# A hand-written order of operations changed in the first four steps, and the last output store split by columns

## The chip, the cores and the metric

The kernel runs on one core of one Trainium2 chip. The metric is the device time of one execution in microseconds (us); the time before is the median of three runs. Five engines work side by side, each through its own queue in order: TensorE (PE in the profile, its weight loads PEld), VectorE (DVE), ScalarE (ACT), GpSimd (POOL) and SyncE (SP), which here only issues DMAs. ACT and POOL issue DMAs too, from the same queues as their other work.

## The reference

```python
f = 1.0 / (1.0 + np.exp(-f_logit))                      # (4, 8, 768, 48)
state = np.zeros((B, H, D, D))
for t in range(S):
    state = f[:, :, t, :, None] * state + einsum('bhd,bhe->bhde', k[:, :, t], v[:, :, t])
    y[:, :, t] = einsum('bhd,bhde->bhe', q[:, :, t], state)
x = y.transpose(0, 2, 1, 3).reshape(3072, 384)
h = x @ w_in                                            # (3072, 2048)
g = np.maximum(h, 0.0) + alpha * np.minimum(h, 0.0)
out = g @ w_out                                         # (3072, 384)
```

All is float32: 4 batches, 8 heads of 48, 768 positions; then a network of width 2048 with a slope alpha for negative values.

## The kernel before

**Steps.** The positions are cut into 6 chunks of 128, the batches into 2 pairs: 12 steps (`STEPS`), each one chunk of one pair, 256 rows of the output. Steps 0 and 1 are the first chunk of the two pairs. In a step three parts are defined as a table of small named operations, `w[name]`: `preparation` (load, sigmoid, products of gates, scaled q and k), `attention` (scores, state, output y) and `network` (the two matrix products).

**Words of the order.** A word stands for one or a few instructions. In `preparation`: `ld.0` to `ld.4` load f, q, k and the two halves of v; `sg`, `kr`, `qc`, `c0` to `c3`, `cg` are ACT's sigmoid and copies; `l1` to `l3`, `le`, `e2` to `e7`, `nr`, `gk`, `k4`, `ke`, `sa`, `sb` are elementwise products on DVE or POOL (all from one helper line, L235); `sc` are scans on DVE, `fs` the factors of the state; `kt` transposes the scaled keys on DVE and `km` moves the pieces with 16 DMAs of SP (L492). `zi` to `zd`, `ci`, `co`, `ch`, `cq`, `cd`, `mr`, `bl` are constants made on POOL. In `attention`: `r` raw scores, `x` scores between groups of four, `h` between halves, `of` blocks off the diagonal, `kp`, `pd`, `pz` key transposes and state products, `y` outputs, `t` the layout of y (all PE); `R`, `X`, `H`, `oc`, `p`, `m`, `z`, `T` copy their results; `mv` moves y into xT by DMA. In `network`: `n0` to `n7` are first-layer products (12 rows of PE each in the profile, `na` and `nb` of step 0 have 24), `g` ACT's negative part, `G` DVE's gates; then seven products by quarters of the second layer, `A1`, `A2`, `B`, `C1`, `C2`, `D`, `E`, over sums of gates `S0`, `S1` and differences of weights `W` (so 7 products in place of 8); `ka`, `u2`, `u3`, `d0`, `oa`, `b`, `d1`, `e` add them up. `d1` and `e` each end with the store of 128 rows of the output. Step 0 has its own network: `na`, `nb`, `ga`, `Ga`, `va`, `vb`, `o`. In step 0, `a` and `b` behind a word mark the two batches of the pair, done apart. `id`, `ih`, `il`, `ib` and `jd`, `jh`, `jl`, `jb` load w_in and w_out in eight pieces each and turn them into the layout of the kernel (DMA, two ACT passes, one DVE sum). `iq`, `ik`, `is`, `ip`, `ix` with a number are products whose results nobody uses.

**The order.** The whole program is one list, `ORDER` (L93): the text `FIRST` for steps 0 to 3 and the parts of steps 3 and 4 that fall between, then `USUAL` repeated for steps 4 to 12, with `+` and `-` for the next and the step before. A word carries its step behind the colon; a last letter V, G or A chooses the engine (DVE, POOL, ACT; for a load the queue of SP, POOL or ACT). The loop at L962 emits the words one after the other, so each engine's queue is the list cut down to its words, and an instruction waits for the tiles that it reads and for the buffers that it takes. The first word on each engine that can't run holds all behind it.

**Buffers.** f, q, k and most tiles of `preparation` have one buffer each (`mine`, `bufs=1`), so a load waits for the last reader of the step before. PSUM: two pairs of banks (`psa`) for scores, state and y, and four single banks (`psn`) for the network; the first of those can be had only when `psf`, the pool of the opening, is given back. Five raw buffers hold pieces of the weights.

The change touches `FIRST` (L31 to L67) and, in `network`, `store`, `oa` and `last`.

## Time and profile before

| what | value |
|---|---|
| runs | 611.93 us median of 3 (611.59 to 613.8) |
| profiled execution | 614.22 us, of it 612.4 us span |
| PE busy | 587.3 us, 96% |
| DVE busy | 488.6 us, 80% |
| ACT, POOL busy | 241.6 and 101.2 us, 39% and 17% |
| chain that ended last | PE 78%, DVE 1% |
| mean granted TensorE clock | 0.986 |
| DMA | 50.41 MB, 82 GB/s mean |

The page cuts the span into 40 slices of 15.3 us; a digit is the busy share in tenths.

```profile
PE   1799899989999999999999999999999999999997
DVE  7978899995857799899899899899889889762251
POOL 4706564364441000000000000000000000000000
PEclk9869999989999999999999999999999999999999
```

POOL works in the first 13 slices alone: the steps of `FIRST` use it for products beside DVE, `USUAL` does not. The clock that the throttle granted is below full in the second, third and ninth slice. Steps of `USUAL` take 46.9 us each (the first `n0` of steps 4 and 5 at 196.36 and 243.21 in the chain of waits). A busy row of PE is not PE at its peak, since its matmuls are pipelined; where it has no gap at all, though, what starts later there ends later.

### The profile page before, as it was taken

What the parts mean: (1) busy time and instruction counts of PE and PEld (TensorE: products, weight loads), DVE (VectorE), ACT (ScalarE), POOL (GpSimd) and SP (SyncE); (2) the same over time, 40 slices, a digit from 0 to 9 for tenths busy, and PEclk for the clock granted to TensorE, in tenths of its full rate; (3) what the DMA queues carried; (4) which work ended last, traced back from release to release, by engine and by line L of the source; (5) the groups of instructions that cost most, each with busy time, mean ns of one, the idle gap of its engine ahead of it and who ended that gap; (6) DMA issues with size and microseconds to landing.
All of it is one profiled execution on the core that took longest, in us unless ns stands there. A gap on an engine that the chain in (4) does not pass through costs nothing.

```text
span 612.4 us, 18785 instructions
## 1 busy us (share of the span) xinstructions
PE 587.3 (96%) x8036; PEld 529.5 (86%) x8036; DVE 488.6 (80%) x996; ACT 241.6 (39%) x461; POOL 101.2 (17%) x141
## 2 busy tenths in 40 slices
PE   1799899989999999999999999999999999999997
PEld 1789857879999899899899899899889889889997
DVE  7978899995857799899899899899889889762251
ACT  5669853414330361272271261261362263223110
POOL 4706564364441000000000000000000000000000
PEclk9869999989999999999999999999999999999999
DMA  8866472223001602502602602502601601201000
GB/s 296 255 208 230 130 232 68 78 47 72 3 29 35 165 8 50 161 2 47 164 1 44 166 2 44 167 1 40 165 7 39 166 7 36 46 3 27 26 1 27
DMA packets 73555, 50.41 MB, mean 82 GB/s; under 512 B 47248, under 2 KB 63120, under 8 KB 73472
## 3 DMA queue, kind: packets, MB, share of 16 engines
q1 hardware_dynamic: 66080, 39.63, 24.2%
q10 hardware_dynamic: 6064, 6.69, 3.7%
q0 software_dynamic: 1328, 2.89, 1.8%
q8 instruction: 64, 1.05, 0.7%
q14 instruction: 19, 0.16, 0.1%
HBM read 36.21 MB, written 4.72 MB: 67 GB/s over the span
## 4 chain that ended last, share of the span: by engine, by line
PE 78%; DVE 1%; issue 0%
PE ph L799 35%; PE pc L894 10%; PE pa L894 9%; PE pe L894 5%; PE pd L894 5%; PE pb L894 4%; PE py L730 3%; PE qu L537 3%; PE raw L517 2%; PE state L655 1%; PE off L617 1%; DVE ss L380 0%; DVE vs L691 0%; DVE o L898 0%; DVE y L739 0%; DVE q L235 0%
## 5 line engine op out<-in xcount | busy, mean ns | idle before, releaser
L799 PE MATMUL ph<-xT,w_in_sb 128*128 128x256 f32 x1056 | 238.0, 384 | 0.0
L799 PEld LDWEIGHTS ph<-xT,w_in_sb 128*128 128x128 f32 x1056 | 199.2, 191 | 29.9 <-issue 1.9
L809 DVE SCALAR_TENSOR_TENSOR gate<-neg,om,ph 128x256 f32<-128x256 f32 x176 | 76.3, 477 | 48.2 <-ACT neg L805 47.0
L805 ACT ACTIVATE neg<-ph 128x512 f32<-128x512 f32 x88 | 51.9, 598 | 158.5 <-PE ph L799 130.4
L767 POOL DMA_DIRECT2D xT<-y x22 | 11.9, 545 | 366.0 <-ACT y L739 366.0
L894 PE MATMUL pc<-t,S 128*128 128x192 f32 x352 | 61.8, 329 | 0.2 <-DVE o L898 0.2
L894 PE MATMUL pa<-w_out_sb,gate 128*128 128x192 f32 x352 | 61.9, 328 | 0.0
L894 PEld LDWEIGHTS pa<-w_out_sb,gate 128*128 128x128 f32 x352 | 57.8, 190 | 1.8 <-DVE gate L809 1.2
L894 PEld LDWEIGHTS pc<-t,S 128*128 128x128 f32 x352 | 57.3, 190 | 1.2 <-DVE o L898 0.5
L544 DVE COPY_PREDICATED ad<-mquad,qu 128x160 f32<-128x160 int32 (+6 forms) x140 | 41.9, 300 | 10.8 <-PE qu L537 5.0
L524 DVE COPY_PREDICATED ad<-mraw,raw 128x128 f32<-128x128 int32 (+3 forms) x96 | 41.6, 442 | 3.8 <-POOL fs L235 0.9
L453 ACT COPY A<-q 48x512 f32<-48x512 f32 x40 | 24.7, 618 | 41.8 <-DVE q L235 41.4
L368 ACT COPY ut<-qd 128x256 f32<-128x256 f32 (+1 forms) x52 | 31.8, 631 | 21.5 <-DVE qd L235 10.2
L235 DVE TENSOR_TENSOR ut<-ut,fs 128x128 f32<-128x128 f32 (+6 forms) x63 | 36.8, 588 | 0.7
L517 PE MATMUL raw<-qd,k 48*32 48x80 f32 x1536 | 23.0, 244 | 13.6 <-DVE qd L235 11.1
L517 PEld LDWEIGHTS raw<-qd,k 48*32 48x32 f32 x1536 | 18.2, 109 | 19.3 <-ACT ut L370 11.1
L917 ACT ACTIVATE o<-pa 128x192 f32<-128x192 f32 x11 | 3.6, 330 | 72.6 <-PE pa L894 72.6
L716 ACT COPY A<-ad 32x256 f32<-32x256 f32 x75 | 30.0, 401 | 2.5 <-DVE ad L544 1.3
L898 DVE SCALAR_TENSOR_TENSOR Csum<-pc,Csum 128x192 f32<-128x192 f32 x22 | 7.9, 357 | 28.6 <-PE pc L894 28.4
L894 PE MATMUL pe<-w_out_sb,S 128*128 128x192 f32 x176 | 30.4, 326 | 0.0
L894 PE MATMUL pb<-t,gate 128*128 128x192 f32 x176 | 30.4, 326 | 0.0
L894 PE MATMUL pd<-w_out_sb,S 128*128 128x192 f32 x176 | 30.4, 326 | 0.0
(138 smaller groups left out, 852.6 us busy)
## 6 DMA issues: line engine op xcount, KB each, us to landing
f<-in_fT SPq DMA_DIRECT2D x11, 512.0 KB, 3.9
w_in_raw<-in_w_in SPq DMA_DIRECT2D x7, 767.2 KB, 7.0
q<-in_qT SPq DMA_DIRECT2D x10, 512.0 KB, 4.9
out<-o SPq DMA_DIRECT2D x24, 192.0 KB, 2.1
k<-in_kT SPq DMA_DIRECT2D x8, 512.0 KB, 7.0
vs<-in_v SPq DMA_DIRECT2D x18, 192.0 KB, 6.9
w_out_raw<-in_w_out SPq DMA_DIRECT2D x4, 767.8 KB, 5.7
w_out_raw<-in_w_out ACTq DMA_DIRECT2D x4, 767.8 KB, 5.6
```

Of the source, the lines that this page charges most:

```text
L235: (nc.gpsimd if beside[0] else nc.vector).tensor_tensor(*a)
L368: w[f"c{r}{mark}"] = lambda r=r: nc.scalar.copy(q4()[:, gs, :, r], qdv[r][:, gs, :, 0])
L453: copy(A[halves(cc)[1], u0:u1, par * HP:(par + 1) * HP, CH * cc:CH * (cc + 1)], x["q3"][rows(par)].rearrange("p (u h c) s t -> p u h c (s ...
L517: nc.tensor.matmul(to[DB * j:DB * (j + 1), par, hp * C:hp * C + QW], lhsT=x["k"][r_, g * DB:(g + 1) * DB], rhs=qd[r_, g], start=True, stop ...
L524: nc.vector.copy_predicated(adu[:, :, :, d:4], mraw[:, d, :, d:4].bitcast(I32).unsqueeze(1).broadcast_to((128, H, NB, n_)), rv[:, :, QO[d] ...
L537: nc.tensor.matmul(to[DB * j:DB * (j + 1), par, o + 4:o + width], lhsT=x["k4"][r_, g * DB:(g + 1) * DB], rhs=x["us"]()[r_, g, 4:width], st ...
L544: nc.vector.copy_predicated(ad[:, u, :, :, 4 * m:DB], mquad[:, lo:lo + n_].bitcast(I32).unsqueeze(1).unsqueeze(1).broadcast_to((128, 2, HP ...
L716: copy(A[s_, u, :, s_], ad[s_, u].rearrange("p r h t -> p (r h) t"))
L799: nc.tensor.matmul(ph[f][:, j * T:(j + 1) * T], lhsT=w_in_sb[:, kt, m * 128:(m + 1) * 128], rhs=x["T"][:, kt], start=(kt == 0 and j == 0), ...
L805: nc.scalar.activation(neg[f], ph[f].rearrange("p (j t) -> p j t", j=2), AF.Relu, scale=-1.0)
L809: nc.vector.scalar_tensor_tensor(gate[:, m % NH, m // NH], neg[f][:, j], om[:, m:m + 1], ph[f].rearrange("p (j t) -> p j t", j=2)[:, j], A ...
L894: nc.tensor.matmul(p[name][:, 0:DH], lhsT=of(f), rhs=by(f), start=(f == 0 and not more), stop=(f == NH - 1), skip_group_check=True)
```

## The change

`FIRST` is replaced by another list of nearly the same words. Of 738 entries, five products without use leave and eight come (`iq.23`, `iq.25`, `iq.27`, `is.8`, `ip.3` against `ik.0`, `ik.2`, `iq.6`, `iq.15`, `iq.22`, `ip.7`, `ix.10`, `ix.11`), and 75 words change engine or queue:

```
step 0: V to G gkb.0 lea nrb.2 sbb.1 sba.1 p01; G to V l3b.0 saa p10; V to A T01 T10 jd7; A to V ldb.3 jd6
step 1: V to G l2.1 ld.3 S0.1; G to V gk.1 ke.0 gk.3 p01 S1.0 S1.1 S1.2; A to V p13 p02; V to A z0; G to A p10; A to G p11
step 2: V to G ld.4 l1.1 l2.0 p13 S0.2 S1.3; G to V l1.0 k4 sb.1 p02 p12 S0.0; A to V p10; A to G p03 p11 p00; G to A ld.2 p01
step 3: V to G k4 sb.1 e2 ld.4 sb.0 p02; G to V ld.2 l1.1 l3.0 sa e5 p13 p01; V to A ld.0 ld.3 z0; A to V p03 z1
step 4: V to G l3.0 k4 le e5 e6; G to V ld.3 l1.1 e3 sa ke.2
```

The rest is shifted places. Below are the parts of the list around the opening, around the products of step 1, and at its end, before and after, then the code.

```diff
@@ -31,40 +31,40 @@
 FIRST = """
-zi:0 ms:0 al:0 zv1:0 zm:0 zk:0 ldb.0V:0 zv0:0 ldb.1V:0 sgb:0 ci:0 l1b.0V:0 l2b.0V:0 mr.2:0 zo.0:0 zf:0 zo.1:0 l3b.0G:0 qcb:0 lda.0V:0 l1b.1V:0 sga:0
-l1a.0V:0 kra:0 krb:0 ldb.2V:0 l2a.0V:0 lda.1V:0 qca:0 l2b.1V:0 zA:0 c2b:0 l3a.0V:0 l1a.1V:0 c0a:0 lda.2V:0 k4aV:0 l2a.1V:0 c2a:0 ch.0:0 sca.1:0 cga:0
-id3A:0 l3b.1V:0 r1:0 k4bV:0 c0b:0 scb.1:0 gka.0V:0 cgb:0 l3a.1V:0 c3a:0 ldb.4V:0 id0V:0 gkb.0V:0 sca.0:0 mr.0:0 id5V:0 bl:0 gkb.1V:0 c1a:0 gka.1V:0
-id4V:0 ih0:0 kea.1V:0 ih5:0 cq.0:0 iq:0 cq.6:0 c1b:0 r0:0 gkb.2V:0 gka.2V:0 cq.4:0 leaV:0 ch.4:0 keb.0V:0 gka.3V:0 h0:0 c3b:0 zd:0 il0:0 kea.0V:0
-lebV:0 gkb.3V:0 H0.0:0 kea.2V:0 nra.0G:0 lda.4A:0 cd.0:0 nrb.0V:0 scb.0:0 sabV:0 sbb.0G:0 keb.2V:0 cd.1:0 keb.1V:0 fs:0 nrb.1V:0 mr.3:0 nrb.2V:0
-ldb.3A:0 nra.1V:0 mr.1:0 sbb.1V:0 nra.2G:0 co:0 h1:0 H1.0:0 H1.1:0 ch.1:0 kpa:0 kpb:0 sba.1V:0 ch.5:0 ch.2:0 il4:0 iq.23:0 H0.2:0 iq.24:0 iq.25:0
-H0.1:0 R0.0:0 ch.3:0 H1.2:0 R1.0:0 R1.1:0 R1.2:0 R1.3:0 ih3:0 cq.1:0 R0.1:0 R0.2:0 kca:0 cd.2:0 ld.0V:1 sg:1 ih4:0 iq.27:0 ld.1V:1 R0.3:0 kcb:0 x1:0
-x0:0 X0.0:0 ofb:0 il3:0 saaG:0 X0.1:0 ofa:0 X1.0:0 qc:1 oc1b:0 is.8:0 ch.6:0 l1.0G:1 pzb:0 lda.3V:0 pza:0 oc0a:0 pda:0 pdb:0 X0.2:0 X1.1:0 p00V:0
-oc1a:0 p02V:0 p01V:0 p03V:0 m0a:0 s10b:0 m0b:0 X1.2:0 oc0b:0 sba.0G:0 s11b:0 l1.1V:1 ip.3:0 s11a:0 p12V:0 s10a:0 bl:1 ib0V:0 y0:0 z0A:0 id1V:0 p11A:0
-il1:0 ih1:0 p13G:0 kr:1 t0:0 T02A:0 jd5A:0 ib4V:0 l2.0V:1 id2V:0 ih2:0 il2:0 id7V:0 T00V:0 p10G:0 y1:0 ib1V:0 T01V:0 na0:0 z1A:0 t1:0 ld.2G:1 l2.1V:1
...
-g4:1 G4.1:1 m1.2:2 G4.0:1 n2:1 ke.1G:3 ke.2V:3 kt:3 km:3 r1:3 R1.0:3 g2:1 W20G:0 r0:3 n1:2 S1.0G:1 S1.2G:1 g1:2 ld.4V:3 n0:2 G3.1:1 e3V:3 e4G:3 e5G:3
-e6G:3 e7G:3 G3.0:1 G2.0:1 G2.1:1 R0.0:3 R1.1:3 R0.1:3 A1:1 ka:1 R1.2:3 R1.3:3 S0.0V:1 S0.1V:1 S0.3V:1 g0:2 sg:4 kr:4 B:1 fs:3 S0.2V:1 G0.0:2 R0.2:3
-R0.3:3 A2:1 n4:2 l1.0G:4 G0.1:2 G1.0:2 x0:3 X0.0:3 qc:4 oa:1 ld.2V:4 l1.1G:4 l2.1G:4 X0.1:3 X0.2:3 S1.1G:1 X0.3:3 X0.4:3 l2.0V:4 G1.1:2 sb.0V:3
-ld.4G:4 x1:3 X1.0:3 C1:1 X1.1:3 S1.3G:1 g4:2 n2:2 X1.2:3 X1.3:3 u2:1 C2:1 G4.1:2 m0.0:3 X1.4:3 X1.5:3 pd:3 X1.6:3 s01:3 p13G:3 of:3 s11:3 c0:4 p11V:3
...
-m1.1:3 e:1 d1:1 ka:2 ke.2G:4 A2:2 z1A:3 u2:2 mv:3 e4V:4 e5V:4 D:2 d0:2 S1.3V:2 E:2 oa:2 e6V:4 S1.2V:2 e7V:4 m1.2:3 C2:2 ke.1G:4 kt:4 km:4 fs:4 u3:2
-b:2 d1:2 e:2 s10:4
+zi:0 ms:0 al:0 cq.0:0 ci:0 zv1:0 ch.0:0 ldb.0V:0 zv0:0 ik.0:0 zf:0 ldb.1V:0 sgb:0 l1b.0V:0 lda.0V:0 qcb:0 l2b.0V:0 l1b.1V:0 zm:0 lda.1V:0 c0b:0 cd.0:0
+cd.1:0 l3b.0V:0 mr.2:0 l2b.1V:0 sga:0 l1a.0V:0 zk:0 l3b.1V:0 kra:0 mr.3:0 cgb:0 lda.2V:0 qca:0 c0a:0 zA:0 gkb.0G:0 zo.0:0 l2a.0V:0 zo.1:0 l3a.0V:0
+l1a.1V:0 ldb.2V:0 r1:0 cga:0 gka.0V:0 id3A:0 lda.4A:0 id0V:0 sca.0:0 l2a.1V:0 l3a.1V:0 r0:0 iq:0 gka.1V:0 c2a:0 k4aV:0 c3a:0 scb.1:0 krb:0 k4bV:0
+c3b:0 mr.0:0 bl:0 sca.1:0 kea.1V:0 c2b:0 c1a:0 leaG:0 mr.1:0 zd:0 id5V:0 gka.2V:0 gka.3V:0 ih5:0 h0:0 c1b:0 iq.24:0 lebV:0 keb.0V:0 ch.1:0 gkb.1V:0
+nrb.1V:0 nra.0G:0 gkb.2V:0 kea.0V:0 gkb.3V:0 H0.0:0 ldb.4V:0 ik.2:0 ih0:0 il0:0 nrb.0V:0 nrb.2G:0 ch.3:0 keb.1V:0 H0.1:0 id4V:0 il4:0 H0.2:0 h1:0
+H1.0:0 kea.2V:0 scb.0:0 ldb.3V:0 keb.2V:0 cd.2:0 sabV:0 nra.1V:0 cq.6:0 fs:0 R0.0:0 R0.1:0 R0.2:0 ih3:0 ld.0V:1 sbb.0G:0 H1.1:0 iq.6:0 ch.6:0 ch.5:0
+kpa:0 sbb.1G:0 H1.2:0 ch.4:0 kpb:0 kca:0 kcb:0 R1.0:0 R1.1:0 sg:1 saaV:0 s11b:0 R1.2:0 iq.15:0 R0.3:0 nra.2G:0 s10b:0 ld.1V:1 sba.0G:0 sba.1G:0 R1.3:0
+iq.22:0 x1:0 x0:0 ch.2:0 X0.0:0 X0.1:0 s11a:0 X0.2:0 p02V:0 il3:0 ib0V:0 lda.3V:0 ofb:0 X1.0:0 X1.1:0 ih4:0 co:0 qc:1 ofa:0 oc0a:0 s10a:0 pzb:0 p00V:0
+p03V:0 pza:0 pda:0 id1V:0 pdb:0 X1.2:0 m0a:0 oc1a:0 oc0b:0 oc1b:0 l1.1V:1 p11A:0 m0b:0 p10V:0 p01G:0 cq.4:0 p12V:0 ib4V:0 ip.7:0 l1.0G:1 y0:0 z0A:0
+il1:0 ix.10:0 ix.11:0 ih1:0 t0:0 T00V:0 cq.2:0 p13G:0 y1:0 ib1V:0 c0:1 T01A:0 jd5A:0 l2.0V:1 id2V:0 ld.2G:1 T02A:0 na0:0 ih2:0 ib3V:0 l2.1G:1 z1A:0
...
+e7V:2 saV:2 ke.0V:2 mv:1 qc:3 x1:2 cq.7:0 sb.1V:2 jl7:0 ke.2V:2 jh7:0 jb7V:0 x0:2 X0.0:2 L:0 kt:2 X0.1:2 X0.2:2 X0.3:2 X0.4:2 l1.0G:3 l1.1V:3 c1:3
+m1.1:1 X1.0:2 X1.1:2 X1.2:2 va3:0 n7:1 l2.0G:3 c0:3 ld.3G:2 km:2 sb.0G:2 s10:2 s00:2 W00V:0 fs:2 vb3:0 ld.4G:2 n0:1 l3.0V:3 sc.1:3 n5:1 W01V:0 o1:0
...
+leV:3 s11:2 n3:1 p11G:2 oc0:2 y1:2 y0:2 e2G:3 n4:1 z1A:2 z0A:2 saV:3 G7.0:1 n2:1 m1.0:2 m1.1:2 m1.2:2 mv:2 W21V:0 e3V:3 g6:1 G6.1:1 G6.0:1 g4:1 g3:1
+e4G:3 ld.4G:3 G4.1:1 G3.0:1 G4.0:1 e5V:3 S1.0V:1 e6G:3 W20G:0 g2:1 r0:3 r1:3 R1.0:3 R1.1:3 sb.0G:3 R0.0:3 R0.1:3 R1.2:3 n1:2 n0:2 G3.1:1 G2.1:1 G2.0:1
+e7G:3 A1:1 ld.1V:4 qc:4 ka:1 B:1 A2:1 ke.2V:3 fs:3 x0:3 S1.1V:1 S0.0V:1 x1:3 R0.2:3 ke.1G:3 kt:3 R0.3:3 S0.1G:1 ld.3A:3 n2:2 ld.2V:4 n4:2 S0.3V:1
+S0.2V:1 g1:2 G1.0:2 G1.1:2 sg:4 g0:2 c0:4 sb.1G:3 R1.3:3 W31V:0 X1.0:3 X1.1:3 X0.0:3 l1.1V:4 s00:3 s11:3 X1.2:3 l2.1G:4 l3.1G:4 X1.3:3 X1.4:3 X1.5:3
+oa:1 C1:1 X0.1:3 X1.6:3 km:3 pd:3 S1.3G:1 g2:2 X0.2:3 G2.1:2 G2.0:2 S1.2V:1 X0.3:3 X0.4:3 g4:2 G0.1:2 of:3 G4.0:2 G4.1:2 X0.5:3 X0.6:3 p00G:3 p13V:3
+l1.0G:4 u2:1 p02G:3 l2.0V:4 oc0:3 W30G:0 G0.0:2 n3:2 C2:1 u3:1 n5:2 b:1 c3:4 l3.0G:4 sc.0:4 c2:4 g3:2 G3.0:2 S0.2G:2 D:1 c1:4 G3.1:2 m0.0:3 g5:2 n6:2
...
+saV:4 p03V:3 sb.0V:4 d0:1 e:1 A1:2 oc1:3 B:2 e2V:4 sb.1V:4 e3V:4 e4V:4 s10:3 y0:3 y1:3 z0A:3 ka:2 s10:4 z1V:3 S1.1G:2 S0.3V:2 S1.3G:2 S1.2V:2 e5G:4
+ld.3V:4 s11:4 C1:2 A2:2 u2:2 C2:2 mv:3 e6G:4 e7V:4 d1:1 s01:4 kr:4 k4G:4 ke.0G:4 oa:2 m1.0:3 m1.1:3 ke.1G:4 s00:4 m1.2:3 D:2 u3:2 d0:2 b:2 d1:2
+ke.2V:4 kt:4 E:2 e:2 km:4 ld.4G:4 fs:4
 """
@@ -840,9 +840,9 @@
             w[f"g{f}"] = lambda f=f: negative(f)
             several(w, f"G{f}", [lambda f=f, j=j: gates(f, j) for j in range(2)])
 
-        def store(u, o):
+        def store(u, o, cols=slice(0, DM)):
             t0 = ((U * bp + u) * NC + c) * C
-            nc.sync.dma_start(out=out[t0:t0 + C], in_=o)
+            nc.sync.dma_start(out=out[t0:t0 + C, cols], in_=o[:, cols])
 
         if plain:
             po = {}
@@ -914,7 +914,14 @@
         w["ka"] = lambda: nc.scalar.activation(kept(), p["a"][:, 0:DH], AF.Copy, scale=UP)
         w["u2"] = lambda: plus(u2(), p["c"], kept())
         w["d0"] = lambda: plus(o(0)[:, DH:DM], p["d"], u2())
-        w["oa"] = lambda: nc.scalar.activation(o(0)[:, 0:DH], p["a"][:, 0:DH], AF.Copy, scale=UP)
+        ends = n == len(steps) - 1
+
+        def left():
+            nc.scalar.activation(o(0)[:, 0:DH], p["a"][:, 0:DH], AF.Copy, scale=UP)
+            if ends:
+                store(0, o(0), slice(0, DH))
+
+        w["oa"] = left
         w["u3"] = lambda: plus(u3(), p["c"], kept())
         w["b"] = lambda: plus(o(1)[:, 0:DH], p["b"], u3(), -UP)
 
@@ -923,7 +930,7 @@
                 plus(o(1)[:, DH:DM], p["d"], u3())
             else:
                 plus(o(0)[:, DH:DM], p["e"], o(0)[:, DH:DM])
-            store(u, o(u))
+            store(u, o(u), slice(0 if u or not ends else DH, DM))
 
         w["d1"], w["e"] = lambda: last(1), lambda: last(0)
```

In step 11, the last of them, `oa` now also stores the left 192 columns of the first batch's rows, and `e` stores the right 192; in all other steps each store is 384 columns wide as before.

## The prediction

> **What bounds the kernel now.** First the windows, cut where the binding engine changes. Columns: stretch, its length, busy us (and instructions) of PE, PEld, DVE, ACT, POOL, granted clock, DMA share, GB/s.

> ```profile
> 0.00:36.30 36.30, 19.83 (x476) 17.38 (x477) 27.87 (x69) 22.68 (x50) 19.25 (x51) 0.87 0.78 252
> 36.30:133.70 97.40, 92.35 (x1479) 76.69 (x1479) 91.21 (x164) 55.56 (x99) 47.73 (x50) 0.96 0.49 147
> 133.70:200.00 66.30, 66.13 (x773) 61.74 (x773) 46.92 (x102) 18.94 (x35) 25.64 (x24) 1.00 0.16 35
> 200.00:612.40 412.40, 409.02 (x5313) 373.67 (x5311) 322.62 (x663) 144.40 (x278) 8.60 (x16) 1.00 0.24 60
> ```

> From 133.7 on PE is busy without a pause (66.13 of 66.30, 409.02 of 412.40 with the drain), so there every us that the start of product `A1` of step 1 moves is a us of the total. Before it DVE decides: adding its idle gaps over 0.15 us one by one gives 3.95 us of idle in 36.3 to 133.7. So the time is: a head until xT of step 0, then DVE's queue up to the last gate of step 1, then PE alone, then the tail. The rows at the joints:

> ```profile
> 31.85 1.98 PE L730 MATMUL py<-A,vs 128*64 128x64 f32 x32
> 34.57 2.93 PE L753 MATMUL xt<-y,dense 128*128 128x128 f32 x12 [0.74 <-ACT y L739]
> 35.90 0.29 DVE L758 COPY xT<-xt 128x128 f32<-128x128 f32 x1 [3.73 <-ACT w_in_sb L267]
> ...
> 122.36 3.76 DVE L235 TENSOR_TENSOR kh<-k,ss 128x512 f32<-128x512 f32 x1
> ...
> 128.34 1.05 PE L517 MATMUL raw<-qd,k 48*32 48x80 f32 x64 [2.48 <-DVE vs L695]
> 132.36 1.25 DVE L809 SCALAR_TENSOR_TENSOR gate<-neg,om,ph 128x256 f32<-128x256 f32 x3
> ```

> DVE stands still for 3.73 us until `T00V` can run at 35.90. At the other end the last gate of step 1 ends at 133.61 (132.36 + 1.25), PE meanwhile lost 2.48 us at `r0:3`, which waited for `m1.2:2`, then ran cold, and began `A1` at 136.11: 2.5 us after the gate.

> **The head (new order against old).** I read each engine's new queue off the diff and gave every operation the duration of its own row. PE: old `y0` 31.85, `t0` 34.57, `na0` 39.33. What held `y0` was a row of PE pieces that themselves waited: `ofb` at 25.0 for `kcb`, which ACT ran only at 24.37 to 24.95, behind `sg:1` (1.06) and `ih4` (0.88). The new ACT order has `kca`, `kcb` ahead of `sg:1`: after `kpb` (`keb.2` has the same 17.4 us of DVE work ahead as before) they end near 22. `of` then follows `x0` at about 23.3, the state products at 24.5. `y0` next waits for `oc1a` (ACT: 22 + sigmoid 1.06 + `il3` 0.92 + `ih4` 0.88 + `qc` 1.04 + 0.51 + 0.63 + 0.51 = 27.5) and for `p03V` (25.8 us of DVE work ahead, some 28). So `y0` at 28 to 28.5 instead of 31.85; `z0A` behind `m0b` on ACT ends near 30.1; `t0` then; `T00V` at 31.2 instead of 35.90 to 36.19. `T01` and `T02` are on ACT behind `il1`, `ih1`, `c0:1` and end at 33.1 (`T02A` old 37.9). DVE's queue shows the same: `T00V` has 29.8 us of work up to its end, before 31.5, and the 3.73 us of idle go. `T10V`, `T01V` leave DVE too, and the waits of 1.23 and 0.63 us for the first gates have cover: `ga0` is ready at 38, `Ga0.2` comes up at 39.9. Gain on DVE behind the head: from 5.0 us (36.2 to 31.2) down to 0, if the chain is held elsewhere. I take **-3.6**, since the chain now runs over more POOL work: `lea`, `gkb.0`, `nrb.2`, `sbb.1`, `sba.1` and `p01` go there, `l3b.0`, `saa`, `p10` come back. Such pieces are not sure beside a dense DVE:

> ```profile
> 13.70 2.93 POOL L226 COPY mquad<-inq 128x8 f32<-128x8 f32 x2 [4.71 <-DVE inq L193]
> ```

> Two copies that take 0.20 each elsewhere took 2.93, while DVE ran sums of two SBUF tiles back to back; and the `kh` row above took 3.76 against 0.68 for the same form where POOL is quiet, and ended just after POOL's 1.82 us `W20G` (125.55). `leaG` meets the same dense stretch at 13 us: 1.2 to 1.4 us lost there is what I subtract. [...]

> **DVE work up to the last gate of step 1.** Leaves this stretch: the head's 1.73 (`lea` 0.68, `sba.1` 0.57, `sbb.1` 0.28, `gkb.0` 0.20), `nrb.2`, `p01`, `T01`, `T10`, `p13:2` 1.41, `l2.1:1`, `l1.1:2`, `l2.0:2`, `z0:1` 3.11, `k4:3`, `sb.1:3`, `e2:3` 2.93, and by order alone `W31`, `ke.2:3`, `kt:3` 2.88: 12.05. Comes in: `l3b.0`, `saa`, `p10` 1.19, `gk.1:1`, `gk.3:1`, `ke.0:1` 1.61, `l1.0:2`, `k4:2`, `sb.1:2`, `l1.1:3`, `l3.0:3`, `sa:3` 5.46, `e5:3`, `S1.0:1` 1.23, six puts 1.71, four `R` copies of step 3 1.73: 12.95 with rounding. **+0.9**; DVE has no cover here, so it is paid. Last gate: 133.6 - 3.6 + 0.9 = 130.9.

> **From the gate to A1.** `m1.0`, `m1.1`, `m1.2` of step 2 now stand together ahead of `W21V`, and `r0:3`, `r1:3` behind `g2:1`, so the wait of 2.48 goes; PE then has to deliver `vb3`, three `n`, `pd`, `of` and so on behind `jb7V`, which moves to 93.7 us of DVE work, so it will wait there instead. The distance of 2.5 us can fall to 0.1 or stay. I take 0.9: `A1` at 131.8, **-4.3** against 136.1.

> **Two prices behind it.** Both are `km`, sixteen SP issues for which a state product waits:

> ```profile
> 193.49 12.65 SPq L492 DMA_DIRECT2D ksn<-kt  x16
> 206.24 1.01 SPq L845 DMA_DIRECT2D out<-o  x2
> 208.73 0.94 PE L655 MATMUL state<-vs,ksn 64*48 64x48 f32 x64
> ```

> The issues took 10.4, 11.0 and 12.65 us (steps 2, 3, 4), landing 2.0 later by the median. Step 4: old `km` starts 1.1 us before PE ends the last product (194.6), lands near 208.2, and `pd` follows at 208.73, half a us of slack. New: `d1:2`, `e:2` and their stores come first on SP, `kt:4` behind `d0`, `b`, `d1`, so `km:4` starts 1.45 us after that product, 2.5 later. With 11 to 12.65 us of issue, PE waits 0.4 to 2.1 us: **+0.9**. Nothing gives it back, since PE is the bound there. Step 3: `kt:3` falls behind the gates by 4.4 us, copies land 17.5 us after the gate; `pd:3` comes up after `A1`, `B`, `A2`, x0, x1, two `n`, `C1`: 3 x 2.60 + 1.86 + 5.2 + 2.6 = 17.5. Between 0 and +1.7, as it has no slack left of 12.9: **+0.4**.

> **No cost of their own.** Three more idle products, 0.4 each warm (`state<-gate` x2: 0.79 cold), lie in PE's waits of the head (1.81, 1.26 and 1.07 us between 13.8 and 26.7); without that cover 1.3. `y0:3`, `y1:3` two products later: xT still has 13 us of products until `n0:3`. The loads: `ldb.2` goes out sixth on SP instead of fourth, 0.95 us later (3.08 against 2.13), and `r1`, which DVE lets go at 7.8, may wait for it until 9; it ran at 11.13 before. Three loads go to ACT (`ld.2:2`, `ld.0:3`, `ld.3:3`), two leave it (`ldb.3`, `jd6`), one swaps in (`jd7`); POOL gets three and gives three. One issue is 0.34 to 0.68 on ACT, 0.64 to 0.90 on POOL, and ACT is busy 55.6 of 97.4 us in the dense stretch. `ld.0A:3` waits on ACT for `le:2`; behind it stands `ga3:0`, whose gates come 3.7 us after `le:2` on DVE. Without that cover, 0.6 (`ga3`) on DVE.

> **The tail.**

> ```profile
> 607.50 2.31 SPq L845 DMA_DIRECT2D out<-o  x2
> 609.06 0.36 DVE L898 SCALAR_TENSOR_TENSOR o<-pe,o 128x192 f32<-128x192 f32 x1 [1.59 <-PE pe L894]
> ```

> The last store is issued at 609.49, its 128 packets of 1536 B move in 0.68 us (610.31 to 610.99), and it lands at 611.34. Half the bytes: at most 0.34 off, at least nothing; **-0.3**. The other half goes out at 604.2, with SP free until 607.50, so the added issue (0.35) is hidden; behind 607.5 it would cost that 0.35.

> **Sum**: -4.3 + 0.4 + 0.9 - 0.3 = -3.3 us, on a span of 612.4 (the profiled execution's time is 614.2). The runs shown have a median of 611.93, so **608.6 us**; its own range is 605.5 to 611.0.

> **Rivals.** (1) *The clock stays up in the head.* Now it is half for four windows:

> ```profile
> 26.59:30.00 3.41, 3.31 (x61) 2.97 (x63) 3.26 (x8) 1.33 (x7) 1.90 (x5) 0.50 0.98 326
> 36.83:40.24 3.41, 3.41 (x40) 3.07 (x39) 3.38 (x6) 2.48 (x5) 0.00 (x0) 0.50 0.75 231
> ```

> `y0` and `t0` then halve (1.98 to 1.0, 2.93 to 1.5): up to 2.4, of which 1.7 reach `T00V`: 606.9. For it: nine idle products instead of six, off starting earlier. Against: between `kpb` and `y0` there are three instead of six. Chance 0.15. [...]
> (2) *Head gain hidden*: POOL's chain holds `y0` at its old time. Then 608.6 + 3.6 = 612.2. Chance 0.12.
> (3) *Slower: DVE and POOL block each other more.* [...] Price: the head's 3.6 lost to a starved POOL, and one more collision like `kh` (3.76 - 0.68 = 3.1) in a stretch with 3.95 us of idle: 608.6 + 6.7 = 615.3. It decides once it takes over 3.3 us more than I allow. For it: DVE rows above the quartile of their form already lose 11 us between 60 and 140. Against: POOL's work in the first steps does not grow (95.6 to 96.1). Chance 0.28.
> (4) The half store saves nothing: 608.9, within my case.

> **How the numbers follow.** My case 0.45: 0.37 of it faster by over 0.5% (under 608.9), 0.08 within. With rival 1, faster is 0.52; with rival 2, within is 0.20; slower 0.28. A difference of 0.5% (3.1 us) is about what a measurement of this kernel tells from none: its three runs spread over 2.2 us. Range 605.0 to 615.3: from beyond rival 1 to the middle of rival 3, leaving out some 0.07 below and 0.13 above.

> **What will show it.** `T00V` near 31 to 33 and no DVE wait of 3.73; `na0` before 36; the last gate of step 1 near 131 and `A1` close behind; a PE wait of 0.4 to 2 us at `pd:4`, less at `pd:3`; the last packets of 768 B. I am wrong if `T00V` stays at 36, if DVE has idle or rows of 2 us and more between 36 and 130, or if PE shows waits of over 1 us between `A1` of step 1 and step 4 anywhere but at the state products.

## The result

Before the change the time was 612.88 us (median of 6 runs, 611.59 to 614.45), after it **608.57 us** (607.46 to 610.44): a ratio of 0.9931, 95% interval 0.9906 to 0.9955. The forecast was 608.6. The two profiled executions took 614.22 and 610.44 us, the second being the longest of its six; their spans are 612.44 and 608.66, 3.78 apart.

The profile after, first the windows of the prediction (columns: stretch, its length, busy us and instructions of PE, PEld, DVE, ACT, POOL, granted clock, DMA share, GB/s):

```profile
0.00:36.30 36.30, 21.76 (x540) 19.48 (x541) 30.23 (x70) 26.55 (x57) 21.90 (x53) 1.00 0.86 272
36.30:133.70 97.40, 92.88 (x1454) 77.69 (x1453) 88.66 (x175) 52.13 (x92) 47.23 (x48) 0.96 0.48 142
133.70:200.00 66.30, 65.81 (x887) 61.13 (x886) 50.17 (x104) 17.57 (x33) 27.70 (x23) 1.00 0.18 39
200.00:608.70 408.70, 403.69 (x5168) 369.37 (x5166) 318.88 (x654) 143.88 (x277) 8.60 (x16) 1.00 0.23 59
```

The first 36.3 us hold 540 products instead of 476. The granted clock, on record from 23.2 us on in both, stays at 1.00 there, where it fell to 0.50 at 26.59 before. DVE's busy time between 36.3 and 133.7 fell from 91.21 to 88.66. Then the joints, from the timeline (start, length, engine, line, operation, and in brackets the idle time before it and what ended it):

```profile
28.49 1.19 PE L730 MATMUL py<-A,vs 128*64 128x64 f32 x28 [0.31 <-ACT A L636]
...
31.21 1.60 PE L753 MATMUL xt<-y,dense 128*128 128x128 f32 x12 [0.89 <-ACT y L739]
...
32.02 0.29 DVE L758 COPY xT<-xt 128x128 f32<-128x128 f32 x1 [1.09 <-PE xt L753]
...
62.10 0.91 PE L537 MATMUL qu<-ut,k 48*32 48x52 f32 x51 [1.82 <-issue]
...
68.81 0.86 DVE L828 SCALAR_TENSOR_TENSOR gate<-neg,om,ph 128x128 f32<-128x128 f32 x3 [2.50 <-ACT neg L823]
...
115.13 0.68 DVE L235 TENSOR_TENSOR kh<-k,ss 128x512 f32<-128x512 f32 x1
...
123.53 1.59 PE L517 MATMUL raw<-qd,k 48*32 48x80 f32 x128
...
128.63 1.23 DVE L809 SCALAR_TENSOR_TENSOR gate<-neg,om,ph 128x256 f32<-128x256 f32 x3
...
130.34 2.76 PE L894 MATMUL pa<-w_out_sb,gate 128*128 128x192 f32 x16
```

`T00V` begins at 32.02 (35.90 before), with 1.09 of DVE's wait of 3.73 left. `kh` takes 0.68 instead of 3.76; POOL stands idle beside it, from 114.23 to 117.53. `r0:3` and `r1:3` run as one row without the wait of 2.48. The last gate ends at 129.86, and `A1` of step 1 begins at 130.34: 5.77 earlier than before. PE's stop of 1.82 at 62.10, for which the profile names no releaser, has its like before (1.90 at 64.59); new are the clock at 0.50 around it, from 60.74 to 67.57, and the 2.50 of DVE idle behind it. DVE also waits 1.42 at 114.34, just ahead of `kh`.

Behind `A1`, on PE and on SP:

```profile
190.55 12.56 SPq L492 DMA_DIRECT2D ksn<-kt  x16
...
204.61 0.89 PE L655 MATMUL state<-vs,ksn 64*48 64x48 f32 x58 [0.83 <-DMA ksn<-kt]
205.43 0.76 PE L617 MATMUL off<-q,kh 48*32 48x32 f32 x64
...
394.75 5.56 PE L799 MATMUL ph<-xT,w_in_sb 128*128 128x256 f32 x25 [1.06 <-issue]
```

PE waits inside `pd:4`, as forecast: `r0:4` came 5.54 earlier than before (189.04 against 194.58), `off:4` only 4.17 (205.43 against 209.60), so 1.37 were given back there. At `g0:4` the lead is 4.25 (241.78 against 246.03). One more stop, of 1.06 at 394.75, takes 0.8 of that: the end of `e:11` comes 3.44 earlier, and the tail adds 0.33.

```profile
600.77 5.56 SPq L845 DMA_DIRECT2D out<-o  x3
...
605.62 0.36 DVE L898 SCALAR_TENSOR_TENSOR o<-pe,o 128x192 f32<-128x192 f32 x1 [1.58 <-PE pe L894]
```

The three issues of the last outputs are one row from 600.77 to 606.33; the last goes out behind `e:11`, whose end at 605.98 lies 2.68 ahead of the end of the span (3.02 before).

### The profile page after: what moved, and what is told of

It reads as the page before. It is cut to its first block, busy times and chain, and to the rows that moved or that the text cites. A ratio compares the mean times of both kernels' runs of the same rounds, so it can differ in the third digit from the quotient of the medians.

```text
span 608.7 us, 18786 instructions
## 1 busy us (share of the span) xinstructions
PE 584.1 (96%) x8042; PEld 527.7 (87%) x8042; DVE 487.9 (80%) x1000; ACT 240.1 (39%) x458; POOL 105.4 (17%) x140
## 3 DMA queue, kind: packets, MB, share of 16 engines
q8 instruction: 64, 1.05, 0.7%
## 4 chain that ended last, share of the span: by engine, by line
PE 88%; DVE 4%; DMA 4%; SPq 2%; issue 1%; ACT 1%; ACTq 0%; DVEq 0%
PE ph L799 36%; PE pc L894 10%; PE pa L894 9%; PE pd L894 5%; PE pe L894 4%; PE pb L894 4%; PE py L730 4%; PE po L859 3%; PE qu L537 3%; PE raw L517 3%; SPq L492 2%; PE ph L817 2%; DMA w_in_raw<-in_w_in 2%; PE state L655 2%; PE off L617 1%
## 5 line engine op out<-in xcount | busy, mean ns | idle before, releaser
L799 PEld LDWEIGHTS ph<-xT,w_in_sb 128*128 128x128 f32 x1056 | 198.2, 190 | 30.5 <-issue 2.7
L809 DVE SCALAR_TENSOR_TENSOR gate<-neg,om,ph 128x256 f32<-128x256 f32 x176 | 76.0, 476 | 48.2 <-ACT neg L805 47.8
L894 PE MATMUL pc<-t,S 128*128 128x192 f32 x352 | 61.7, 329 | 0.0
L894 PE MATMUL pa<-w_out_sb,gate 128*128 128x192 f32 x352 | 61.7, 328 | 0.0
L894 PEld LDWEIGHTS pa<-w_out_sb,gate 128*128 128x128 f32 x352 | 57.9, 190 | 1.6 <-DVE gate L809 0.9
L894 PEld LDWEIGHTS pc<-t,S 128*128 128x128 f32 x352 | 57.4, 190 | 0.7
L544 DVE COPY_PREDICATED ad<-mquad,qu 128x128 f32<-128x128 int32 (+6 forms) x140 | 41.5, 299 | 5.9 <-PE qu L537 0.5
L524 DVE COPY_PREDICATED ad<-mraw,raw 128x256 f32<-128x256 int32 (+3 forms) x96 | 41.5, 445 | 2.8 <-PE raw L517 0.6
L235 DVE TENSOR_TENSOR ut<-ut,fs 128x128 f32<-128x128 f32 (+7 forms) x61 | 34.9, 574 | 1.1 <-POOL ut L235 0.4
L898 DVE SCALAR_TENSOR_TENSOR Csum<-pc,Csum 128x192 f32<-128x192 f32 x22 | 7.9, 357 | 31.2 <-PE pc L894 31.0
L894 PE MATMUL pb<-t,gate 128*128 128x192 f32 x176 | 30.4, 326 | 0.0
L894 PE MATMUL pe<-w_out_sb,S 128*128 128x192 f32 x176 | 30.4, 326 | 0.0
L894 PE MATMUL pd<-w_out_sb,S 128*128 128x192 f32 x176 | 30.4, 326 | 0.0
L517 PE MATMUL raw<-qd,k 48*32 48x80 f32 x1536 | 22.9, 243 | 7.0 <-DMA k<-in_kT 6.7
L517 PEld LDWEIGHTS raw<-qd,k 48*32 48x32 f32 x1536 | 18.3, 109 | 12.9 <-ACT ut L370 7.0
L235 DVE TENSOR_TENSOR S<-gate 128x512 f32<-128x512 f32 x42 | 28.9, 688 | 0.6
```

The lines of the kernel that those rows point to most:

```text
L235: (nc.gpsimd if beside[0] else nc.vector).tensor_tensor(*a)
L517: nc.tensor.matmul(to[DB * j:DB * (j + 1), par, hp * C:hp * C + QW], lhsT=x["k"][r_, g * DB:(g + 1) * DB], rhs=qd[r_, g], start=True, stop ...
L524: nc.vector.copy_predicated(adu[:, :, :, d:4], mraw[:, d, :, d:4].bitcast(I32).unsqueeze(1).broadcast_to((128, H, NB, n_)), rv[:, :, QO[d] ...
L544: nc.vector.copy_predicated(ad[:, u, :, :, 4 * m:DB], mquad[:, lo:lo + n_].bitcast(I32).unsqueeze(1).unsqueeze(1).broadcast_to((128, 2, HP ...
L799: nc.tensor.matmul(ph[f][:, j * T:(j + 1) * T], lhsT=w_in_sb[:, kt, m * 128:(m + 1) * 128], rhs=x["T"][:, kt], start=(kt == 0 and j == 0), ...
L809: nc.vector.scalar_tensor_tensor(gate[:, m % NH, m // NH], neg[f][:, j], om[:, m:m + 1], ph[f].rearrange("p (j t) -> p j t", j=2)[:, j], A ...
```

## The experiments

Each kernel was timed beside runs of the kernel before, whose median lay between 613.5 and 614.1 us; ratios are to those. Line numbers of these kernels are 3 lower (L514 for L517), as their order is set in fewer rows. No run has the head of the one order with the rest of the other, so no run prices the two parts of the new order apart.

**The two prices behind A1.** `e1_tail_only` is the old order with the split store.

> The kernel before, order unchanged, with the split last store alone. Theory (the forecast's tail term): 0.30 us shorter, at most 0.34: the last packets are 768 B instead of 1536 B and land about 0.3 earlier behind e:11, the other half is issued near 604 and costs nothing. Rival: the last store's fixed part sets its end, 0.0. Either is too small for the times (about -0.05%); it is read from the distance between the end of e:11 on DVE and the end of the span, 3.0 us in the kernel before.

The time was 614.72 against 613.72, a ratio of 1.001 (0.9989 to 1.0032): no difference that the times can show. From the end of `e:11` to the end of the span it is 2.69 us; it is 3.02 before, 2.68 after, and 3.0 in each of the kernels below with the old store. The term of 0.3 stands.

`e2_km4_early` changes the new order only:

```diff
- ... m1.2:3 D:2 u3:2 d0:2 b:2 d1:2 ke.2V:4 kt:4 E:2 e:2 km:4 ...
+ ... m1.2:3 ke.2V:4 kt:4 km:4 D:2 u3:2 d0:2 b:2 d1:2 E:2 e:2 ...
```

> The kernel after with ke.2V:4, kt:4 and km:4 ahead of D:2, so that the sixteen copies of step 4 go out on SP ahead of the two stores of step 2 instead of behind them. Theory: the wait at pd:4 (PE stood from 203.7 to 204.6, and off:4 came 1.37 us late) is km's place alone. ke.2 can run when POOL's kh is there (186.6), kt ends near 189.0, km goes out from about 189.2 instead of 190.55 and its last copy lands before PE comes to pd:4: the whole 1.37 us come back, 607.2 against 608.57 (-0.2%), with the product off:4 near 204.1 instead of 205.43. Rival: the copies are held by the queue and not by their start, or the adds u3, b, d1 that now come behind kt hold a bank for r0:4: then off:4 stays at 205.4 or r0:4 slips by up to 0.8, and the time is 608.6 or above.

The time was 608.27, a ratio of 0.9917 (0.9884 to 0.9949); the times cannot tell it from the kernel after. The wait for the copies is gone, and another has come into the same place:

```profile
200.36 0.94 PE L652 MATMUL state<-vs,ksn 64*48 64x48 f32 x64
201.22 0.59 PE L614 MATMUL off<-q,kh 48*32 48x32 f32 x44
202.49 0.38 PE L614 MATMUL off<-q,kh 48*32 48x32 f32 x20 [0.68 <-issue]
```

`pd:4` runs as one row; 20 products short of the end of `off:4` PE stops for 0.68. From `A1` of step 1 to `g0:4` it is 110.95 against 111.44 in the kernel after: of 1.37 only 0.5 came through. The price was `km`'s place, as the theory has it; the new stop belongs to the next question.

**PE's stops without a releaser.** Where nothing in the profile ended a wait of PE, its row has `<-issue`. `e4_no_idle` leaves the nine idle products out of the new order: nine words whose results nobody uses, each of them two products with their weight loads, 36 instructions of PE in all.

> The kernel after without any of its nine idle products of step 0. Theory 1 (the forecast's own: they lie in PE's waits and cost nothing, and the order alone brings the head's gain): T00V stays within 0.4 us of 32.0, time 608.2 to 609.0. Theory 2 (rival 1 of the forecast, they keep the granted clock at 1.00): the clock falls to 0.50 for one to four windows of 3.4 us between 16 and 40, the state products go from 1.50 back to 2.5 us, t0 from 1.60 to 2.9, T00V comes 1.5 to 2.5 later, at 33.5 to 34.5, and the time is 609.5 to 611.

The time was 616.79, a ratio of 1.0049 (1.0025 to 1.0074): over 7 us more than the kernel after, and neither theory gives that. `T00V` was at 32.41, `A1` at 129.96, the last adds of step 2 at 189.2, all within 0.4 of the kernel after. The time goes at one place in step 4:

```profile
203.56 0.89 PE L652 MATMUL state<-vs,ksn 64*48 64x48 f32 x58 [0.30 <-DMA ksn<-kt]
204.37 0.74 PE L614 MATMUL off<-q,kh 48*32 48x32 f32 x62
209.73 0.26 PE L614 MATMUL off<-q,kh 48*32 48x32 f32 x2 [4.62 <-issue]
```

Two products short of the end of `off:4` PE stops for 4.62 us. The transfers of that stretch (203 to 209.8 us, GB/s in 40 equal slices; then the queue, its packets, MB and share):

```profile
GB/s 14 0 217 72 0 0 24 193 337 398 398 386 458 410 386 410 422 398 398 398 434 398 422 410 494 373 386 361 361 341 395 370 283 202 220 211 220 220 57 51
...
q8 instruction: 1, 0.02, 0.9%
```

The inputs of step 5 move at 340 to 490 GB/s for most of it, and among them is one packet on queue 8, of kind instruction: 16 KB, landing at 208.26. PE goes on at 209.73. Over the whole run that queue carries 63 packets (64 after) for 8024 products with as many weight loads: one for 255 of PE's instructions. I compared every stop of PE of 0.6 us or more without a releaser, in all fourteen profiles, with the last such packet ahead of it: all 35 ended 1.19 to 1.56 us after one had landed (one more, of 0.63 at 9.28 in `e4`, lies ahead of the first packet). The place fits too. Numbered in the trace, with the sequencer's own, PE's instruction behind each of the 35 stops is number 193 or 194 behind a multiple of 256; and at none of the 881 such places in the fourteen profiles did PE go on sooner than 1.19 us after the packet's landing. So I read these as waits for **PE's own code**: the profile names the packets as instructions, and the place of a stop goes with the count of PE's instructions. Most of the packets were in time: of some 64 a run, two to four were waited for by 0.6 us or more; but one stop of 0.9 to 2.0 us stands near 60 us in every profile.

`e5_idle_first` puts the nine back, all in front of `r1:0`; nothing else changes.

> The kernel after with its nine idle products all ahead of r1 of step 0, where PE waits for its first input anyway, and none later. The kernel without any of them (616.8) kept the gain up to the last product of step 2 and then lost 4.6 us in one stop inside off:4, to which the profile gives no releaser; the 16 KB packet of PE's instructions that lands there (207.2 to 208.2) comes between the four input loads of step 5. Theory: PE stops because it has run through the code it holds, and where it does is set by the number of its instructions ahead; nine idle products are 36 of them. With the nine at the front the count ahead of off:4 is that of the kernel after, so the stop of 4.6 is gone: g0:4 within 3 us of 241.8 instead of 248.5, time 608.5 to 611.5 (the clock of the head is lost as it was without them, 1 to 2 us against 608.57). Rival: the stop belongs to what the idle products do to the head (its clock, its order in time): then it stays, 615 to 617.

The time was 607.95, a ratio of 0.9919 (0.9888 to 0.9951), a little under the range of the theory. The stop of 4.62 is gone (`g0:4` 238.00), and a stop is back at 391 (0.94), at the same instruction as in the kernel after. Of the 10.5 us between the two kernels at `g0:4`, 4.1 are there at `A1` already; 6.4 come with the stop: its 4.6, and the clock, which falls to 0.50 behind it (the next 48 products `ph` take 13.48 in `e4`, 10.63 after). So 36 instructions in the head, where they cost nothing, decide over 6 us in step 4. `e7_km4_less3` is `e2` without `ik.0`, `ix.10`, `ix.11`, 12 instructions fewer:

> The version with km:4 ahead of D:2 (608.27 median, span 605.3 in its profile), without the three idle products ik.0, ix.10, ix.11, so that PE's instruction count behind step 0 is that of the kernel before. Theory (PE stops where its stored code ends): the stops without a releaser at 202.5 (0.68) and 391.3 (0.94) go, as the kernel before has none behind 70 us, and the product that follows e:2 to the last one take 1.0 to 1.6 us less; T00V is later by at most 0.5; time 606.3 to 607.3. Rival: those stops are not tied to the count (they are the loads' alone): they stay, and the time is 608 to 609.

The time was 606.64, a ratio of 0.9897 (0.9862 to 0.9931); the interval overlaps that of `e2`, so the gain is read from the traces. Behind 72 us there is no stop, as the theory has it, but one of 1.21 at 71.32 is new, and `T00V` is 2.06 later than in `e2` (32.58 against 30.52), not 0.5. From `A1` to `g0:4` it is 110.22 (111.44 after), so now 1.2 of the 1.37 came through, and from the end of `e:2` to that of `e:11` it is 412.83 against 414.39 in `e2`. `e10_km4_six_first` keeps that count and moves the six that remain to the front:

> The version with km:4 ahead of D:2, with six idle products, all ahead of r1 of step 0 (the count of the version without ik.0, ix.10, ix.11: 606.64 median, span 604.9). Theory: only the count matters behind the head, so again no stop without a releaser behind 80 us, and from g0:4 to e:11 the same 362.7 us; in the head the clock opens near 20.6 and falls again at 27.4 as with nine first, T00V near 31 to 32.5; time 606 to 607.5. Rival: the idle products between 16 and 27 us are needed to open the clock: PE stays at half speed until 34 as without any (T00V 32.4 or later, on PE's rows 2.93 for t0), and the time is 607.5 to 609.

The time was 608.43, a ratio of 0.9917 (0.9888 to 0.9945): the theory missed. `off:4` in `e7`, and then here:

```profile
202.47 0.76 PE L614 MATMUL off<-q,kh 48*32 48x32 f32 x64
...
202.49 0.64 PE L614 MATMUL off<-q,kh 48*32 48x32 f32 x50
205.05 0.32 PE L614 MATMUL off<-q,kh 48*32 48x32 f32 x14 [1.91 <-issue]
```

With the same count there is a stop of 1.91 at 205.05, where `e7` has none: the packet that landed at 198.42 there landed at 203.60 here. Its rival was right on the clock, which rose only at 36.76. In these runs the count says after which product PE can run out; when the packet lands says whether it does. What held that packet up here no run shows.

**What held the head.** The prediction blamed `kcb`. `e3_old_kcb` moves it alone, in the old order:

```diff
- ... kca:0 cd.2:0 ld.0V:1 sg:1 ih4:0 iq.27:0 ld.1V:1 R0.3:0 kcb:0 ...
+ ... cd.2:0 ld.0V:1 kca:0 kcb:0 sg:1 ih4:0 iq.27:0 ld.1V:1 R0.3:0 ...
```

> The kernel before with one move: the two copies kca, kcb ahead of sg:1 and ih4 in ACT's order (two tokens). Theory (the forecast's first step in the head): kcb's late place held ofb and so y0. kcb then ends near 23.0 instead of 24.95, off runs without its pauses of 1.26 and 1.07 us, PE does not lose its clock at 26.6, and y0 starts 1.5 to 2.5 us earlier than 31.85, T00V up to 3 earlier than 35.90; DVE takes over what it can, and the time falls by 1.0 to 3.0 us, 610 to 612. Rival: POOL and DVE rows further down (p03V at 29.4, z0 on ACT behind the last A copies) hold y0 anyway: T00V within 0.5 us of 35.9 and the time as before, 612.9.

The time was 613.64, a ratio of 1.0007 (0.9981 to 1.0033): no gain. `kcb` ended at 22.52 instead of 24.95. First the kernel before, then this one:

```profile
25.00 0.62 PE L627 MATMUL off<-q,kh 48*64 48x64 f32 x13 [1.26 <-ACT ksn L599]
26.69 1.33 PE L627 MATMUL off<-q,kh 48*64 48x64 f32 x19 [1.07 <-issue]
...
23.21 0.62 PE L624 MATMUL off<-q,kh 48*64 48x64 f32 x13
26.87 0.80 PE L624 MATMUL off<-q,kh 48*64 48x64 f32 x19 [3.04 <-issue]
...
33.60 2.93 PE L750 MATMUL xt<-y,dense 128*128 128x128 f32 x12 [0.74 <-ACT y L736]
```

`off` starts 1.8 earlier, stops after the same thirteen products as before, and resumes at 26.87 (26.69 before): the code had landed at 25.4 in both. I had read the pause of 1.07 in the kernel before as `kcb`'s doing. `e8_old_fill` put four idle products into the wait for `kcb`:

> The kernel before with four more idle products of step 0 just ahead of ofb, where PE waits 1.26 us for kcb. Theory (rival 1 of the forecast as a cause of its own): the granted clock falls to 0.50 at 26.6 because PE was busy for only 1.15 of the 3.4 us before; with the wait filled it stays at 1.00, the state products take 1.50 instead of 2.53, t0 1.6 instead of 2.93, T00V comes 1.5 to 2.2 earlier than 35.9, DVE hands on 1.0 to 2.2 of it, time 610.7 to 612. Rival: filling a wait is not enough, since the second pause of off (1.07, no releaser) stays: the clock falls at 26.6 as before, T00V at 35.9 to 36.3, time 612.9 or up to 0.4 more.

The time was 614.73, a ratio of 1.0011 (0.9989 to 1.0033). `off` stopped after four products for 2.31, the clock fell at 29.26, and `T00V` began at 35.89. The rival held, through the code again: with sixteen more instructions ahead the stop comes earlier in `off`, and there is another, of 1.51 at 398.62, where the kernel before has none.

`e9_lea_V` tests the 1.2 to 1.4 us that I subtracted for `lea` on POOL:

> The kernel after with lea of step 0 on DVE instead of POOL (one token, leaG:0 to leaV:0). Theory (the forecast subtracted 1.2 to 1.4 us of the head's gain for it): on POOL it takes 1.64 us in all runs of the new order against 0.69 on DVE, and DVE stood 1.91 us at leb for it; back on DVE, leb starts 0.5 to 1.2 us earlier and the head gets shorter by as much: from p03V's end to T00V's end no longer than 4.3 us, T00V 0.5 to 1.2 earlier than in the kernel after (32.0, between 30.5 and 32.6 in its relatives), time 607.4 to 608.1. Rival: the 0.7 us more on DVE are paid where the dense queue counts, and leb's wait is for the transfers, not for POOL: T00V same or later by up to 0.7, time 608.6 to 609.3.

The time was 609.20, a ratio of 0.9931 (0.9899 to 0.9962), the same ratio as the kernel after. From the end of `p03V`, DVE's last copy ahead of `y0`, to the start of `T00V` it is 3.98 us, 4.00 in the kernel after: the rival. On POOL `lea` saves DVE its 0.68, and the DVE row beside it (`ks`) takes 1.30 instead of 0.42, so the trade is even. The wait of 1.91 at `leb` ends with ACT's copy into `ut`, not with POOL: it is 0.55 here, and 0.75 in `e10` with `lea` on POOL.

Now the code itself. In the kernel before, its packet lands at 25.44 behind a burst of transfers (300 to 410 KB in each us from 19 to 24); after, the burst is later and thinner (72 to 294 KB in each us from 18 to 22, 403 and 238 in the two behind), and it lands at 23.97. `e11_old_code` takes the load `id1` from SP to ACT, on top of `e3`:

```diff
- ... kca:0 cd.2:0 ld.0V:1 sg:1 ih4:0 ... R0.3:0 kcb:0 ... id1V:0 ...
+ ... cd.2:0 ld.0V:1 kca:0 kcb:0 id1A:0 sg:1 ih4:0 ... R0.3:0 ...
```

> The kernel before with kca, kcb ahead of sg:1 and ih4, and with the load id1 (767 KB) on ACT behind kcb instead of on SP at 18.0: three tokens. With kcb early alone, off stopped 3.04 us behind its thirteenth product until PE's next 16 KB of code had landed (25.4, as in the kernel before), at the end of a burst of 300 to 400 KB a us from 18.6 to 24; T00V moved by 0.98. Theory: the code packet is held by that burst. With id1 out of it the burst ends about 2 us sooner, the code lands between 22.8 and 24.2, off is done by 25 to 26 instead of 27.7, y0 begins at 28.5 to 30, T00V at 32.5 to 34, and A1 of step 1 comes 1.5 to 3 us earlier than in the kernel before; time 610.5 to 612.5 against 613.5 to 614. Rival: the packet comes at its own time (PE asks for it late): it lands at 25.2 or later, T00V at 34.9 or later, the time as before.

The time was 608.16 against 613.84, a ratio of 0.9914 (0.9882 to 0.9946), better than the range of the theory. `id1` went out at 19.67 instead of 18.01: ACT issued it ahead of `kca` and `kcb`, which stand before it in the list and ran from 21.14, so the rule that the first word that can't run holds all behind it does not cover this DMA issue. The packet landed at 23.73, and the clock stayed at 1.00 from 20.78 to 58:

```profile
22.37 0.62 PE L624 MATMUL off<-q,kh 48*64 48x64 f32 x13
25.09 0.79 PE L624 MATMUL off<-q,kh 48*64 48x64 f32 x19 [2.10 <-issue]
...
28.09 1.47 PE L727 MATMUL py<-A,vs 128*64 128x64 f32 x32
...
31.56 0.29 DVE L755 COPY xT<-xt 128x128 f32<-128x128 f32 x1
```

`T00V` begins at 31.56, even before that of the kernel after, without one of its trades between engines. From `p03V`'s end (27.5 to 28.0 in all four) to `T00V`'s start it is 7.9 us before, 7.1 with `kcb` alone, 4.1 with `kcb` and the load, 4.0 after. Of the 3.36 us that the load brought at `T00V`, 1.78 are there when `off` resumes. The other 1.6 come with the clock, which fell at 28.45 in `e3` and stays up here (the 64 state products take 1.51 instead of 2.21); `e1`, whose head is that of the kernel before, shows the packet alone: it landed 0.66 later there (26.09), and `T00V` began 0.72 later (36.62), with the clock as before.

**The dense stretch.** `e6_old_W20_late` moves one POOL sum in the old order.

```diff
- ... km:3 r1:3 R1.0:3 g2:1 W20G:0 r0:3 n1:2 S1.0G:1 S1.2G:1 g1:2 ...
+ ... km:3 r1:3 R1.0:3 g2:1 r0:3 n1:2 S1.0G:1 S1.2G:1 W20G:0 g1:2 ...
```

> The kernel before with W20G:0 (POOL's 1.82 us sum at 123.73) behind S1.2G:1, one token moved. Theory: DVE's kh (ke.0V:3) takes 3.76 us because it and POOL's ks and W20G keep each other off; it holds m1.1, m1.2 of step 2 and so r0:3 on PE (wait of 2.48). Without W20G beside it kh takes at most 1.6 (until ks ends, 1.14) and the wait at r0:3 falls below 0.5, A1 of step 1 comes 1.8 to 2.2 us earlier than 136.1 (or than the same distance of 99.9 from T00V), time 610.7 to 611.2 against 612.9. Rival: kh is slow by itself or because of the transfers, or the gates hold A1 anyway: kh stays above 3 us, A1 unchanged, 612.9.

The time was 611.05 against 614.09, a ratio of 0.9955 (0.9933 to 0.9976). First POOL's sum in the kernel before, beside `kh`'s row of 122.36 to 126.11, then this kernel:

```profile
123.73 1.82 POOL L235 TENSOR_TENSOR t<-t,w_out_sb 128x768 f32<-128x768 f32 x1
...
123.30 1.97 DVE L232 TENSOR_TENSOR kh<-k,ss 128x512 f32<-128x512 f32 x1
...
127.49 0.92 PE L514 MATMUL raw<-qd,k 48*32 48x80 f32 x64 [0.70 <-DVE vs L692]
...
133.62 2.76 PE L891 MATMUL pa<-w_out_sb,gate 128*128 128x192 f32 x16
```

`kh` falls to 1.97, the wait at `r0:3` to 0.70, and the clock no longer drops behind it (3.41 us at half before): `A1` comes 2.49 earlier, with `T00V` where it was. From the start of `kh` to `A1` it is 10.32 us instead of 13.75, but `kh` starts 0.94 later than before. So the collision costs 3.4 us where it happens, 2.5 at `A1` in this trace, and 3.0 by the medians. Last, `e12_old_code_W20` is `e11` with this move too:

> The same with W20G:0 behind S1.2G:1 too: the old order with four tokens moved against the two things that the traces name, the code packet in the head and the collision of kh with W20G (2.6 us at A1 in the trace, 611.05 against 614.09 in the times). Theory: the two add, since they lie in the two halves of DVE's queue: A1 of step 1 at 131 to 132.5 against 136.1 and 130.3 in the kernel after; time 608.0 to 610.0. Rival: what the head hands on is lost again before the gates, or the head doesn't move: 610.5 to 611.5, as with W20G alone.

The time was **604.58** us (603.67 to 606.37) against 613.84, a ratio of 0.9858 (0.9829 to 0.9887): better than forecast, and better than the kernel after (0.9931, 0.9906 to 0.9955; the intervals don't meet).

```profile
0.00:36.30 36.30, 21.15 (x539) 18.59 (x540) 31.97 (x75) 25.93 (x55) 19.26 (x51) 1.00 0.84 271
36.30:125.90 89.60, 86.59 (x1428) 71.40 (x1427) 86.94 (x162) 52.74 (x94) 48.91 (x50) 1.00 0.51 153
```

The second stretch ends where `A1` of step 1 begins, at 125.89, 10.2 earlier than before; the clock is 1.00 there, on record from 22.27 on, and DVE is busy for 86.94 of its 89.60 us. At `A1` the two moves alone gave 2.3 (`e11`) and 2.5 (`e6`). The rest lies mostly at 58 us: in `e11` PE stopped there for 1.84, the clock was at 0.50 for the 6.83 us behind it, and DVE stood 3.28 at 66.4; here the stop is 0.88 and the clock stays. The profile of `e11` is of its longest execution (611.88), so the traces overstate that part; by the medians the second move brought 3.6. What makes the stop at 58 shorter stays open.

## Why the prediction was right, and where it was not

The direction and the path were right, but the total was met by errors that cancel, and the match to the last digit is luck. The sum was -3.3 us from 611.93; against the 612.88 of six runs the change is -4.31, and between the two spans -3.78. What follows compares one profiled execution of each kernel: among the seven profiles of the new order and its variants, that of the kernel after has the longest way from `T00V` to `A1` (98.32, the others 94.76 to 97.55). By the prediction's own steps:

- *What bounds the kernel*: held. `T00V`, then DVE's queue to the last gate, then PE; the 5.77 gained at `A1` reached the end but for the 1.37 at `pd:4` and the stop at 394.75, to within 0.2.
- *The head*, -3.6 forecast, **-3.87** measured. The size was right, the cause in the main wrong: "What held `y0` was a row of PE pieces that themselves waited: `ofb` at 25.0 for `kcb`". In the old order `kcb` alone gives 1 us at `T00V` (`e3`); taking a load out of the burst ahead of the code packet gives the rest, partly through the clock (`e11`). That the new order moves loads away from 17 to 18 us (`lda.4` and `ldb.3` go out at 7.8 to 8.6, `ld.1` and `id1` at 19.7 and 20.7) I had costed at nothing. No run puts these loads back in the new order, so that they carry its gain is argued from the old one. The 1.2 to 1.4 subtracted for `lea` is not there either (`e9`).
- *DVE's work*, +0.9 forecast, last gate -2.7; measured **-3.76**, the head's gain less 0.1. The failed term is the 3.76 of `kh`, which I carried over as it stood: in the new order it is 0.68, and `e6` prices the collision at 2.5 at `A1`. Against it stands a loss that I had not listed: the 6.83 us of half clock around the code stop at 62.10, with 1.23 and 2.50 of DVE idle. From `T00V` to the last gate DVE is busy 2.9 us less than before (88.5 against 91.4) and idle 3.0 more (9.3 against 6.3). An idle time of over 2 us there was among the prediction's own signs of being wrong.
- *Gate to `A1`*: 0.9 forecast, 0.49 measured (2.50 before); the clock, at 0.50 from 128.99 to 132.40 before, stays up here. `A1` -4.3 forecast, **-5.77** measured.
- *`pd:3`*: 0.4 forecast, 0. *`pd:4`*: 0.9 (0.4 to 2.1) forecast, **1.37**; `e2` and `e7` show that it is `km`'s place and that 0.5 to 1.2 of it can be had back.
- *The idle products* at no cost: true for the nine as they stand, but for the wrong reason. Their number moves the product of `off:4` behind which PE stops: the 44th with nine (`e2`), the 50th with six (`e10`), the 62nd with none (`e4`). Leaving them out costs over 7 us (`e4`), and 12 instructions fewer take a stop away in step 4 (`e7`).
- *The tail*: -0.3, measured -0.33.
- *Behind `A1`*: no other loss was forecast; the code stop at 394.75 took 1.06, of which 0.8 are left at the end.

Rival 1 came true and was worth little by itself in the new order: the clock stays up to 60.74 in the kernel after, but where it fell at 27.4 or 29.5 (`e5`, `e7`) the way from `p03V` to `T00V` was the same 4.0; with PE at half clock up to 34.8 or 36.8 (`e4`, `e10`) it was 6.6 and 4.7. Rival 2 did not come: POOL holds `y0` in some variants (1.6 to 1.8 us for `mquad` in `e5`, `e7` and `e9`), but at 26.95 to 28.41, not at the old 31.85. Nor did rival 3: `kh`'s collision is gone, and the new one beside `lea` costs DVE 0.9, of which `lea`'s own 0.68 comes back. What makes DVE and POOL slow each other no run shows.

## What to carry over

A wait with no releaser is a finding, not a remainder (35 of the 36 over 0.6 us here ended 1.19 to 1.56 us behind a packet of instructions): set it beside the packets of the instruction queue, and look at which loads run then, before blaming the nearest late operand. A row far over its form's usual time may be a removable cost (`kh` took 3.76 us, and 1.97 with one POOL sum moved): ask what ran beside it before carrying it into a sum. And before reordering hundreds of words, look for the few places that the traces name: four words moved in the old order beat all of the new one by 4 us.
